# Attention with landmarks and a gated MLP: the first two loads on the hardware queues in the other order

## The chip, the cores and the metric

The kernel runs on one core of one Trainium2 chip. The metric is the device time of one execution in microseconds (us); lower is better. Of the core, the text speaks of TensorE (PE, matrix products and transposes; PEld is its weight load), VectorE (DVE), ScalarE (ACT), GpSimd (POOL) and SyncE (SP). SP and ACT each issue transfers on a hardware queue of their own, POOL on a software queue; all three queues are served by the same 16 DMA engines.

## The reference

For each of 8 batches and 8 heads, 32 landmark rows `p` attend to 576 keys and values, and the 576 queries attend to the 32 rows that come out. The result is the input of two matrix products with a gate between them.

```python
def sm_attn(qq, kk, vv):
    s = scale * np.matmul(qq, kk.transpose(0, 1, 3, 2))
    s = s - np.max(s, axis=-1, keepdims=True)
    a = np.exp(s)
    a = a / (np.sum(a, axis=-1, keepdims=True) + 1e-09)
    return np.matmul(a, vv)
p_packed = sm_attn(p, k, v)
out = sm_attn(q, p_packed, p_packed)
...
h = x @ w_in                      # 4608 x 512 by 512 x 2048
g = np.where(pos, h, np.where(neg, 0.0, (h + beta) ** 2 / (4.0 * beta)))
return (g @ w_out).astype(np.float32)
```

## The kernel before

The work goes batch by batch. For a batch: keys and queries are turned so that the head's 64 channels lie on the partitions; the landmarks' scores against the keys (`sp`), their exponentials (`ex`), the packed values and their sums (`pk`, `ppT`, `rs`); the queries' scores against the packed rows (`s`), exponentials (`eT`), sums (`sm`), logarithm and reciprocal (`ln`, `rc`) and the scaled probabilities (`A`). The packed rows are multiplied with `w_in` directly (`mp`, copied to `M`), so that the hidden layer (`h`, line 939) is a product of `M` and `A`; the gate is three steps on ACT and DVE (`x`, `t`, `hT`), and `w_out` gives the output (`o`, line 1030), which is copied to `ob` and stored. All output tiles and all hidden layers are spread over the time of the batches around them.

The order of the instructions on each engine is written out by a planner in the program (`Plan`): each step has a rank, the engines that can do it with an estimated occupancy and duration, steps that it depends on, and buffers that it takes. `plan.run` walks through time with these estimates and gives one list, in which each engine's instructions are then emitted in that order. Most ranks stand in a table (`RANKS`), by the step's name. Where the planned PE has nothing to do before the first output product, matmuls on a tile of zeros (`zeros`, line 1108) are put in; their number is fixed when the program is built. They are called fillers below. An engine works through its own list in order and waits at each instruction for what it needs.

The change touches the start of batch 0. Three kinds of loads begin there:

- On SP's and ACT's hardware queue, one half each: `p_raw`, the float32 landmarks of batches 0 and 1 (line 485, 64 KB on each queue, in runs of 256 bytes), and `k_raw`, the float32 keys of batch 0, heads 0 to 3 (line 491, 288 KB on each queue, in runs of 1536 bytes). SP brings heads 0 and 1, ACT heads 2 and 3.
- On POOL's queue, with a cast to bf16 on the way: the keys of heads 4 to 7 (line 444), then the values, queries and weights.

`p_raw` is cast by DVE to `p_nat` (line 537), turned on PE into `tpp` (line 515, eight small transposes) and copied to `pT` by ACT and DVE, two copies each. `k_raw` is cast by DVE (heads 0 and 1) and ACT (heads 2 and 3), both at line 333, into the bf16 keys. The keys of batch 0 lie in a buffer that is later used for `M`, so **the rows call the keys of batch 0 `M` too**. PE turns them in two steps of twelve transposes (line 564, `tp`): heads 0 to 3, then heads 4 to 7. Each step is copied to `kT` by ACT (one copy of 384 columns) and DVE (one of 768). The scores `sp` are two steps of twelve matmuls (line 667) of `kT` with `pT`, one after each half of `kT`; ACT makes `ex` of each (line 676). After the scores come seven fillers and then `pk` (line 735).

Of the kernel before, what the change touches and what calls it, by code (L numbers as in the profile page):

```python
# [130 lines left out]
def kernel(  # L131
# [193 lines left out]
    plan = Plan(dict(BUFS, dma=8), RANKS)  # L325
# [15 lines left out]
    def either(dve, act, *pairs, parted=None):  # L341

        def emit(e):
            for to, of in pairs:
                copy(e, to(), of(), parted)
        return {"DVE": (dve[0], dve[1], emit), "ACT": (act[0], act[1], emit)}
# [137 lines left out]
        for i, queue in enumerate((nc.sync, nc.scalar)):  # L484
            queue.dma_start(p_raw[:, i], p[i].rearrange("h n d -> n h d"))

    p_first = plan.add(-1000, {"SP": (1.0, 3.5, load_p_raw)})

    def load_k_raw(e):
        for i, queue in enumerate((nc.sync, nc.scalar)):  # L490
            queue.dma_start(k_raw[:, 2 * i:2 * i + 2], rows_of("k", 0, range(2 * i, 2 * i + 2)))

    k_first = plan.add(-999, {"SP": (1.0, 4.75, load_k_raw)}, behind=[p_first])
    casts = [plan.add(-30.2 + 0.1 * i, either(
        (0.5, 0.55), (0.8, 0.85), (lambda i=i: tokens("k", 0)[:, 2 * i:2 * i + 2], lambda i=i: k_raw[:, 2 * i:2 * i + 2])),
        [k_first], behind=landed["k", 0, 4]) for i in range(2)]
# [647 lines left out]
```

## Time and profile before

| | |
|---|---|
| time, median of 3 runs | 241.79 us (241.51 to 241.95) |
| profiled execution: its time, its span | 242.18 us, 240.4 us |
| PE busy | 233.2 us, 97% of the span |
| ACT busy | 190.0 us, 79% |
| DVE busy | 179.4 us, 75% |
| POOL busy | 37.7 us, 16% |

The span runs from the first to the last instruction of the profiled execution; its time is 1.78 us longer, for what lies around it. Busy PE counts pipelined matmuls with ends that are modelled. All times in the rows are from the start of the span.

### The profile page before, as it was taken

The numbers are of one execution on the slowest core, as the hardware profiler recorded it, in microseconds if no ns is written. First come the engines' busy times: TensorE is split into PE (matmuls) and PEld (weight loads), VectorE is DVE, ScalarE is ACT, GpSimd is POOL, SyncE is SP. The second block draws the span as 40 slices with busy tenths as digits, with TensorE's granted clock in tenths as the row PEclk, the third lists the DMA queues.
The fourth block names the chain that finished last, engine by engine and source line by source line (L and its number), as shares of the span: only waits on it lengthen the run. The fifth ranks groups of instructions, "written<-read, shape, count | busy, mean of one in ns | idle before, by whom it ended". The sixth has DMA issues, their size and how long they took to land.

```text
span 240.4 us, 5315 instructions
## 1 busy us (share of the span) xinstructions
PE 233.2 (97%) x2096; PEld 133.9 (56%) x2096; DVE 179.4 (75%) x320; ACT 190.0 (79%) x324; POOL 37.7 (16%) x57
## 2 busy tenths in 40 slices
PE   7799999999999999999999999999999999999993
PEld 3555565565555655466546655656456554654452
DVE  4549997499977996699868989999469967995000
ACT  3578898799989986899889898998789886984211
POOL 8552306000510040070005000300000000000000
PEclk9999999999999999999999999999999999999999
DMA  7999999999999999999999997989301210111315
GB/s 155 201 206 207 203 202 206 199 257 171 148 188 248 186 171 204 187 174 213 204 183 197 218 213 117 138 189 203 97 2 48 74 33 27 44 40 52 98 45 119
DMA packets 65353, 36.42 MB, mean 152 GB/s; under 512 B 34480, under 2 KB 60848, under 8 KB 65328
## 3 DMA queue, kind: packets, MB, share of 16 engines
q0 software_dynamic: 28080, 18.26, 53.5%
q1 hardware_dynamic: 36544, 17.28, 33.4%
q10 hardware_dynamic: 704, 0.56, 0.8%
q8 instruction: 16, 0.26, 0.4%
q14 instruction: 9, 0.07, 0.1%
HBM read 37.22 MB, written 9.44 MB: 194 GB/s over the span
## 4 chain that ended last, share of the span: by engine, by line
PE 92%; ACT 3%; DMA 2%; DVE 1%; issue 0%
PE o L1030 51%; PE h L939 26%; PE mp L792 3%; DMA k_raw<-in_k_dram 2%; PE o L1108 2%; PE pk L730 2%; PE sm L835 2%; PE sp L652 2%; PE s L770 1%; PE tp L564 1%; ACT M L333 1%; PE pk L740 1%; DVE M L333 0%; ACT rc L846 0%; PE tp L601 0%; PE sp L667 0%
## 5 line engine op out<-in xcount | busy, mean ns | idle before, releaser
L1030 PE MATMUL o<-w_out_sb,hT 128*128 128x512 bf16 (+1 forms) x592 | 146.3, 374 | 0.0
L960 DVE SCALAR_TENSOR_TENSOR hT<-t 128x576 bf16<-128x576 f32 (+1 forms) x130 | 91.9, 742 | 3.7 <-ACT t L955 2.1
L945 ACT ACTIVATE x<-h 128x576 f32<-128x576 f32 (+1 forms) x130 | 79.2, 646 | 11.6 <-PE h L939 10.7
L1030 PEld LDWEIGHTS <-hT 128*128 128x128 bf16 x592 | 55.3, 98 | 49.3 <-issue 5.6
L939 PE MATMUL h<-A,M 128*128 128x288 bf16 x512 | 78.1, 286 | 0.6 <-ACT M L333 0.4
L939 PEld LDWEIGHTS <-M 128*128 128x128 bf16 x512 | 49.6, 98 | 27.7 <-issue 1.5
L953 DVE TENSOR_SCALAR t<-x 128x576 f32<-128x576 f32 (+1 forms) x75 | 33.6, 463 | 10.6 <-ACT x L945 10.2
L955 ACT ACTIVATE t<-x 128x576 f32<-128x576 f32 (+1 forms) x55 | 37.0, 684 | 0.9
L333 ACT COPY ob<-o 128x512 f32<-128x512 f32 (+1 forms) x21 | 11.9, 567 | 16.5 <-PE o L1030 16.3
L851 DVE SCALAR_TENSOR_TENSOR A<-eT,rs,rc 128x576 bf16<-128x576 bf16 (+1 forms) x18 | 12.9, 747 | 10.7 <-ACT rc L846 10.7
L333 ACT CAST M<-mp 128x1024 bf16<-128x1024 f32 (+1 forms) x19 | 17.7, 969 | 2.5 <-PE mp L792 2.4
L430 POOL DMA_DIRECT2D v<-in_v_dram x14 | 10.2, 731 | 52.2 <-DVE vz L708 48.9
L430 POOL DMA_DIRECT2D kz<-in_k_dram x14 | 9.7, 701 | 50.9 <-DMA kT<-kz 50.2
L333 DVE CAST M<-mp 128x1024 bf16<-128x1024 f32 (+1 forms) x15 | 17.2, 1147 | 0.4 <-PE mp L792 0.4
L333 DVE COPY ob<-o 128x512 f32<-128x512 f32 x16 | 10.9, 685 | 2.7 <-PE o L1030 2.6
L1108 PE MATMUL o<-zeros 128*128 128x512 bf16 (+1 forms) x42 | 11.4, 405 | 1.2 <-DVE zeros L367 1.2
L828 ACT ACTIVATE eT<-s,rs 128x576 bf16<-128x576 f32 x16 | 11.1, 736 | 1.8 <-PE s L770 1.2
L841 ACT ACTIVATE ln<-sm 128x576 f32<-128x576 f32 x16 | 10.1, 651 | 1.9 <-PE sm L835 1.7
L846 ACT ACTIVATE rc<-ln 128x576 f32<-128x576 f32 (+1 forms) x18 | 10.6, 634 | 0.0
L792 PE MATMUL mp<-w_in_sb,ppT 64*32 64x512 bf16 x256 | 10.3, 380 | 0.0
L674 ACT ACTIVATE ex<-sp 128x640 bf16<-128x640 f32 x14 | 9.5, 702 | 0.3 <-PE sp L652 0.2
L444 POOL DMA_DIRECT2D q<-in_q_dram x11 | 8.4, 762 | 5.1 <-ACT x L945 2.1
(62 smaller groups left out, 110.7 us busy)
## 6 DMA issues: line engine op xcount, KB each, us to landing
out_dram<-ob SPq DMA_DIRECT2D x23, 192.0 KB, 2.7
q<-in_q_dram POOLq DMA_DIRECT2D x7, 576.0 KB, 16.1
out_dram<-ob SPq DMA_DIRECT2D x24, 128.0 KB, 3.9
kz<-in_k_dram POOLq DMA_DIRECT2D x7, 320.0 KB, 6.4
v<-in_v_dram POOLq DMA_DIRECT2D x7, 320.0 KB, 8.6
w_out_sb<-in_moe_w_out_dram POOLq DMA_DIRECT2D x4, 512.0 KB, 15.3
kz<-in_k_dram POOLq DMA_DIRECT2D x7, 256.0 KB, 7.3
v<-in_v_dram POOLq DMA_DIRECT2D x7, 256.0 KB, 9.6
```

What stands on the lines that cost most here:

```text
L333: i = (nc.vector.tensor_copy if e == "DVE" else nc.scalar.copy)(to, of)
L430: return G_.dma_start(tokens(nm, b)[p0:p0 + R5, :, :c * D], of)
L792: i = nc.tensor.matmul(have["mp", b, f][a * NP:(a + 1) * NP, g], have["ppT", b][r, g, a], w_in_sb[r, a, f * FW:(f + 1) * FW], start=True, ...
L828: nc.scalar.activation(have["eT", b, g][:, part], have["s2", b, g][:, part, :HALF], AF.Exp, scale=rs_of[b][:, g, 1:])
L851: V.scalar_tensor_tensor(have["A", b][:, g, part], have["eT", b, g][:, part], rs_of[b][:, g, :1], have["rc", b, g][:, part], ALU.mult, ALU ...
L939: nc.tensor.matmul(have["h", b, fi][:, hf, :HALF], have["M", b][:, g, fi * P:(fi + 1) * P], have["A", b][:, g, hf], start=(g == 0), stop=( ...
L945: nc.scalar.activation(have["x", b, fi][:, hs[0]:hs[-1] + 1], have["h", b, fi][:, hs[0]:hs[-1] + 1, :HALF], AF.Prelu, bias=-1.0, alpha=0.5)
L953: V.tensor_scalar(t, x, 1.0, 0.0, ALU.add, ALU.max)
L955: nc.scalar.activation(t, x, AF.Relu, bias=1.0)
L960: V.scalar_tensor_tensor(dst, t, 1.0, t, ALU.min, ALU.mult)
L1030: m = nc.tensor.matmul(have["o", key][:, :w], hT[:, fi, i * P:(i + 1) * P], w_out_sb[:, fi, cols], start=(fi == 0), stop=(fi == KF - 1))
L1108: nc.tensor.matmul(o[:, :w], zeros[:, :P], zeros[:, :w], start=True, stop=True)
```

## The change

The two loads on the hardware queues change places: the keys are planned and issued first, and the landmarks behind them. The estimated durations of the two loads, which the planner uses, change with it. No transfer, no arithmetic step and no buffer is added or removed; one line less stands in the file, so that line numbers from 489 on are one lower after the change.

```diff
-    p_first = plan.add(-1000, {"SP": (1.0, 3.5, load_p_raw)})
-
     def load_k_raw(e):
         for i, queue in enumerate((nc.sync, nc.scalar)):
             queue.dma_start(k_raw[:, 2 * i:2 * i + 2], rows_of("k", 0, range(2 * i, 2 * i + 2)))
 
-    k_first = plan.add(-999, {"SP": (1.0, 4.75, load_k_raw)}, behind=[p_first])
+    k_first = plan.add(-1000, {"SP": (1.0, 5.0, load_k_raw)})
+    p_first = plan.add(-999, {"SP": (1.0, 4.3, load_p_raw)}, behind=[k_first])
```

The planner then puts some instructions of the first ten microseconds in another order. On ACT, the start of the program read before:

```order
L310 ACT_TABLE_LOAD
L485 DMA p_raw<-in_p_dram 32x8x64
L491 DMA k_raw<-in_k_dram 96x2x384
L333 COPY pT<-tpp 64x8x32 x2
L333 CAST M<-k_raw 96x768
L333 COPY kT<-tp 128x4x96 x2
L676 ACTIVATE ex<-sp 96x12x64 x2
```

After the change ACT reads:

```order
L310 ACT_TABLE_LOAD
L489 DMA k_raw<-in_k_dram 96x2x384
L485 DMA p_raw<-in_p_dram 32x8x64
L333 CAST M<-k_raw 96x768
L333 COPY kT<-tp 128x4x96
L333 COPY pT<-tpp 64x8x32 x2
L333 COPY kT<-tp 128x4x96
L675 ACTIVATE ex<-sp 96x12x64 x2
```

The two copies of `pT` moved from ahead of the cast to between the two copies of `kT`. SP issues the same two loads in the new order too. On DVE, behind the first constants, the rows before were:

```order
L374 MEMSET ones_77 64x1
L537 CAST p_nat<-p_raw 32x1024
L333 COPY pT<-tpp 64x8x32 x2
L333 CAST M<-k_raw 96x768
L333 COPY kT<-tp 128x4x192 x2
```

and are after the change:

```order
L374 MEMSET ones_77 64x1
L333 CAST M<-k_raw 96x768
L536 CAST p_nat<-p_raw 32x1024
L333 COPY kT<-tp 128x4x192
L333 COPY pT<-tpp 64x8x32 x2
L333 COPY kT<-tp 128x4x192
```

The cast of the landmarks now stands behind that of the keys, and the copies of `pT` between those of `kT`. On PE the eight transposes of the landmarks stood ahead of all transposes of keys, behind eight fillers (seven of 512 columns and one of 256) and ahead of six more (five and one). After the change twelve fillers stand at the start, then the twelve transposes of heads 0 to 3, and then the eight of the landmarks with two fillers behind them; this is where these end and heads 4 to 7 begin:

```order
L514 LDWEIGHTS p_nat
L514 MATMUL tpp<-ident,p_nat 128x32
L1107 LDWEIGHTS zeros
L1107 MATMUL o<-zeros 128x512
L1107 LDWEIGHTS zeros
L1107 MATMUL o<-zeros 128x256
L563 LDWEIGHTS M
L563 MATMUL tp<-ident,M 128x96
```

So eight transposes of landmarks and two fillers moved between the two halves of the keys. A single filler of 256 columns, which stood between the last transpose of keys and the first score, stands between the two steps of scores instead. From there on the list of PE is the same, the seven fillers ahead of `pk` included, and so are all of POOL's list and the rest of the others.

## Rows read from the trace of the kernel before

**Rows 1.** Busy time of each engine in one long stretch (us, then instructions).

```profile
19.40:236.00 216.60, 216.03 (x1886) 124.79 (x1885) 169.29 (x290) 178.41 (x301) 25.75 (x35) 1.00 0.87 149
```

**Rows 2.** The chain that ended last: its longest piece before 20 us.

```profile
1.23 5.52 DMA k_raw<-in_k_dram
```

**Rows 3.** Timeline, the first issues of transfers: start, us, engine, line.

```profile
0.74 0.38 SPq L485 DMA_DIRECT2D p_raw<-in_p_dram  x1
0.77 0.42 ACTq L485 DMA_DIRECT2D p_raw<-in_p_dram  x1
1.19 0.43 SPq L491 DMA_DIRECT2D k_raw<-in_k_dram  x1
1.23 0.47 ACTq L491 DMA_DIRECT2D k_raw<-in_k_dram  x1
...
1.30 0.81 POOL L444 DMA_DIRECT2D M<-in_k_dram  x1 [0.85 <-POOLq L1128]
```

**Rows 4.** Transfers: size, and us from issue to landing (last number).

```profile
k_raw<-in_k_dram SPq DMA_DIRECT2D x1, 288.0 KB, 5.3
k_raw<-in_k_dram ACTq DMA_DIRECT2D x1, 288.0 KB, 5.5
M<-in_k_dram POOLq DMA_DIRECT2D x1, 288.0 KB, 6.5
```

**Rows 5.** DMA packets by queue, 2.4 to 2.6 us (q1 SP, q10 ACT).

```profile
q1 hardware_dynamic: 14, 0.02, 88.0%
q10 hardware_dynamic: 46, 0.01, 25.9%
```

**Rows 6.** The same, 5.4 to 7 us (q0 POOL's queue).

```profile
q0 software_dynamic: 424, 0.31, 128.7%
q10 hardware_dynamic: 2, 0.00, 0.4%
```

**Rows 7.** Timeline, 0 to 8 us: fillers, landmarks and the two casts of keys.

```profile
1.19 3.22 PE L1108 MATMUL o<-zeros 128*128 128x512 bf16 x8 [1.19 <-DVE zeros L367]
...
3.38 0.68 DVE L537 CAST p_nat<-p_raw 32x1024 bf16<-32x1024 f32 x1 [0.87 <-DMA p_raw<-in_p_dram]
...
4.34 0.36 PE L515 MATMUL tpp<-ident,p_nat 32*128 32x32 bf16 x8
...
4.63 1.36 PE L1108 MATMUL o<-zeros 128*128 128x512 bf16 x6
4.74 0.75 ACT L333 COPY pT<-tpp 64x256 bf16<-64x256 bf16 x2 [2.72 <-PE tpp L515]
4.74 0.58 DVE L333 COPY pT<-tpp 64x256 bf16<-64x256 bf16 x2 [0.68 <-PE tpp L515]
...
6.49 0.60 DVE L333 CAST M<-k_raw 96x768 bf16<-96x768 f32 x1 [1.17 <-DMA k_raw<-in_k_dram]
6.77 0.83 ACT L333 CAST M<-k_raw 96x768 bf16<-96x768 f32 x1 [1.28 <-DMA k_raw<-in_k_dram]
```

**Rows 8.** Timeline, 6 to 24 us: from the keys to the packed values.

```profile
7.66 1.11 PE L564 MATMUL tp<-ident,M 96*128 96x96 bf16 x22 [0.24 <-ACT M L333]
...
8.29 0.99 ACT L333 COPY kT<-tp 128x384 bf16<-128x384 bf16 x2 [0.69 <-PE tp L564]
8.29 1.07 DVE L333 COPY kT<-tp 128x768 bf16<-128x768 bf16 x2 [1.19 <-PE tp L564]
...
8.90 1.05 PE L667 MATMUL sp<-pT,kT 128*128 128x64 bf16 x24
9.48 1.50 ACT L676 ACTIVATE ex<-sp 96x768 bf16<-96x768 f32 x2 [0.20 <-PE sp L667]
...
9.79 1.68 PE L1108 MATMUL o<-zeros 128*128 128x512 bf16 x7
10.53 0.74 POOL L464 DMA_DIRECT2D w_out_sb<-in_moe_w_out_dram  x1 [1.73 <-DMA v<-in_v_dram]
...
11.40 0.94 PE L735 MATMUL pk<-ex,v 96*64 96x32 bf16 x48
```

## The prediction

> **What bounds the kernel now.** I read the stretches first, then the chain that ended last, then the timeline of the first 12 us, and last the queues. From 19.4 to 236 us PE is busy for 216.03 of 216.60 us [rows 1]: it waits for 0.6 us in nine tenths of the span, so that nothing the change leaves alone can give time back there, and what the first 19 us gain or lose arrives at the end almost one to one. In those first microseconds the chain has one long piece that is no engine's work: 5.52 us for `k_raw` [rows 2]. So the question is when the scores of batch 0 are done, and what stands between them and the load.
>
> Issued at 1.23 us, ACT's half lands 5.5 us later, at 6.73, and SP's half at 1.19 + 5.3 = 6.49 [rows 3, 4]; both casts start within 0.04 us of that [rows 7]. ACT's is the later one. I call its landing a, and count from it: the cast from a + 0.04 takes 0.83 us [rows 7]; ten transposes of heads 0 to 3 that were left follow at 7.66 = a + 0.93, and heads 4 to 7 directly behind, 22 in 1.11 us, so 0.05 us each [rows 8]. The copies of the first half start at 8.29 = a + 1.56, that is 0.13 us after the tenth, and DVE's two end at 8.29 + 1.07 = 9.36 = a + 2.63 [rows 8]. That end holds the second step of scores: 0.43 us later, at 9.79, the seven fillers begin, and `pk` follows them at 11.40 [rows 8]. The exponentials, from 9.48 for 1.50 us, are done at 10.98 and the values were there by 10.53 [rows 8]; so `pk` stands behind scores and fillers, and comes earlier or later with the end of DVE's second copy.
>
> The landmarks are far off this path: cast at 3.38, copied by 5.5 us [rows 7], while the keys come a microsecond later. That slack is what the change spends.
>
> **What the change does to the keys' landing (a).** Each half is issued where the landmarks' half was: 1.19 − 0.74 = 0.45 us earlier on SP and 1.23 − 0.77 = 0.46 on ACT [rows 3]. The keys also waited behind the landmarks' packets: between 2.4 and 2.6 us SP's queue moves packets of keys already (14 packets, 0.02 MB), ACT's still the short ones of the landmarks (46, 0.01 MB) [rows 5], 0.7 us after the keys' issue ended at 1.70. I take 0.55 us for the shift. Of the old queue almost nothing is left after 5.4 us: 2 packets on ACT's [rows 6], yet the landing comes at 6.73, so it trails the last packets by about 1.25 us. The landmarks' last packets went at about 2.6 [rows 5], and their cast began at 3.38 [rows 7]: a trail of under 0.8 us. Between the two, POOL's queue came to full flow (424 packets in 1.6 us [rows 6]). With packets that end near 4.9, a is 4.9 + 0.75 = 5.65 if the trail is the short one and 4.9 + 1.25 = 6.15 if it is the long one; I take the middle, 5.9. Outer bound on the late side: no gain, 6.73.
>
> The Trainium skill, page "DMA: Bandwidth & Descriptors", section "Queues, rings and completion order", says that a completion count is written only after all earlier writes of that DMA engine, across its queues. The two trails fit it: short when the hardware queues are alone, long beside POOL's. By it alone, with POOL's queue hardly begun at 4.9, a would be 5.65 and the keys' term below 0.25 us better; the rows don't separate the engines, and the sum keeps 5.9.
>
> **What it does to the landmarks' landing (b).** They are now last on both queues. The bytes of the two queues are the same, so their last packets go near 5.45 as before, but beside POOL's traffic. With the two trails b is 6.2 to 6.7; POOL's queue is in full flow then, so I go by the longer one and take 6.55. The late bound: 64 KB in runs of 256 bytes are 256 on each queue, 16 for each engine; POOL's 424 packets in 1.6 us [rows 6] are one for an engine every 0.06 us, and if each run lets one of them pass, 16 runs from 4.9 on last until 5.9, and b is up to 7.15.
>
> **What the new order costs.** On PE the landmarks' transposes follow heads 0 to 3, at a + 0.93 + 10 × 0.05 = a + 1.43. Until the next filler they take 4.63 − 4.34 = 0.29 us [rows 7]. The two fillers behind them are 768 columns; six fillers that were 5.5 × 512 columns took 1.36 us with their drain [rows 7], and seven full ones some 1.6 [rows 8], so 0.22 for 512 columns and 0.33 for both. Heads 4 to 7 then start at a + 2.05 instead of a + 1.43, end 12 × 0.05 later at a + 2.65, and can be copied at a + 2.78. DVE has its first copy until a + 1.56 + 0.53 = a + 2.09, the landmarks' copies for 0.58 [rows 7] until a + 2.67, and so is free: its second copy runs to a + 2.78 + 0.53 = a + 3.31, where it was a + 2.63. **The new order costs 0.68 us behind the keys' landing.** ACT: copy, 0.75 us for `pT` [rows 7], copy, so a + 1.56 + 0.5 + 0.75 + 0.5 = a + 3.31; the first scores need `pT` (a + 2.81) and take 9.48 − 8.90 = 0.58, so `ex` starts near a + 3.43 instead of a + 2.75 and ends at a + 4.93 = 10.83, still ahead of `pk`. That one filler moves between the steps of scores costs nothing: DVE's second copy ends later.
>
> If b is late, the landmarks' transposes wait: cast from b + 0.1 for 0.68, 0.06 until PE begins (as 6.49 + 0.60 to 7.15 for the keys), so b + 0.84, and DVE's second copy ends 3.31 − 1.43 = 1.88 later, at b + 2.72. A third wait is that for heads 4 to 7, which POOL brings: issued 1.30, landed 6.5 later at 7.8 [rows 3, 4]. Transposes from 7.85 give an end of 7.85 + 0.6 + 0.13 + 0.53 = 9.11. That load isn't moved by the change.
>
> **The sum.** DVE's second copy ends at the latest of a + 3.31, b + 2.72 and 9.11, against 9.36 now. With a = 5.9 and b = 6.55: 9.21, 9.27 and 9.11, so 9.27, that is 0.09 us earlier. The keys' gain of 0.83 is nearly all paid back by the 0.68 and by the landmarks, which become the last wait. On the profiled execution this makes a span of 240.3 us and a time of 242.1; that execution lies 0.39 above the median, which I take off again: **241.7 us**. Break-even is a = 6.05, b = 6.64.
>
> **The rivals.** 0.2% (0.48 us) is about what a measurement of this kernel can tell from no change.
> - *The landmarks become the long wait.* Decides from b = 6.64 on; b = 7.15 gives 9.87, 0.51 us later, 242.3. For it: short runs at the tail, beside POOL's 0.31 MB. Against it: their trail alone was under 0.8.
> - *The keys don't land earlier*, since POOL's traffic and not their place sets the trail: a between 6.5 and 6.73 gives 0.45 to 0.68 later, 242.4. Against it: nearly all their packets were through before POOL's flow.
> - *All three loads land earlier*, heads 4 to 7 too, because the hardware queues' long packets are out of POOL's way sooner: a = 5.6, b = 6.1, POOL's 0.3 us earlier, an end of 8.91, 241.3. Against it: the old 7.8 us for heads 4 to 7 stands in the way of more than 0.25.
> - *TensorE's clock falls back.* Fillers ran at 3.22/8 = 0.40 us first and at 0.22 from 4.63 on [rows 7], 512 columns at about the 1.2 and the 2.4 GHz level. Twelve fillers in one block end near 5.3, PE then idles until SP's half is cast (near 6.3), and has less to do in the next microsecond than before; before it idled for 1.16 us in the same place and kept its pace. At the lower level the nine fillers behind it (8.5 × 512 columns) cost 8.5 × 0.2 = 1.7 us, with transposes and scores 2.3 and more: 244. The page "TensorE: Matmul & The Clock Gate" of the Trainium skill, Part 1, lets the clock drop after idleness; no stretch of this trace past 4.6 us shows it.
>
> **How the numbers follow.** Forecast (an end within 0.48 us of 9.36 with a and b near the values taken): 0.63, itself 241.4 to 242.0. Landmarks late: 0.13, of which half over 0.48. Keys not earlier: 0.09. All earlier: 0.11. Clock: 0.04. Slower by over 0.2%: 0.06 + 0.09 + 0.04 = 0.19; faster: 0.11 and a little of the forecast's edge, 0.13; within: 0.68. The range, 241.2 to 242.4, holds the forecast and most of the first three rivals.
>
> **What would show it.** Right: `k_raw` landing near 5.7 and 5.9, `p_raw` after it near 6.5, the landmarks' transposes directly behind heads 0 to 3, DVE's second copy ending near 9.3, `pk` near 11.3. Wrong: a landing of `p_raw` past 6.9 or of `k_raw` past 6.3, a landing of heads 4 to 7 far from 7.8, fillers of 0.4 us after 5 us, or a change of the end that the start of `pk` doesn't show.

## The result and the profile after

The changed kernel takes 242.23 us (median of 22 executions, 241.61 to 244.32), the kernel before 241.66 beside it (22, 241.26 to 242.28). The ratio is 1.0031, with an interval of 1.0019 to 1.0043: slower by 0.3%, where 241.7 and no change were forecast (a loss of over 0.2% had a chance of 0.19). The median is 0.57 us higher; the means lie 0.77 apart, because two executions of 22 took over 244 us.

The profiled execution of the changed kernel is the shortest of its 22 (241.61 us, span 239.8), and that of before lies near the top of its range (242.18). Set side by side, these two profiles show a gain that the times don't have. First the issues in the profile after (size, us from issue to landing):

```profile
k_raw<-in_k_dram SPq DMA_DIRECT2D x1, 288.0 KB, 3.5
k_raw<-in_k_dram ACTq DMA_DIRECT2D x1, 288.0 KB, 4.3
M<-in_k_dram POOLq DMA_DIRECT2D x1, 288.0 KB, 6.0
p_raw<-in_p_dram SPq DMA_DIRECT2D x1, 64.0 KB, 4.3
p_raw<-in_p_dram ACTq DMA_DIRECT2D x1, 64.0 KB, 4.7
```

The keys are issued at 0.74 and 0.77 us now, so ACT's half lands at 5.1 (6.7 in [rows 4]); the landmarks, issued at 1.23, at 5.9; heads 4 to 7, issued at 1.30 as before, at 7.3 (7.8). The timeline of the same execution, which answers to [rows 7, 8]:

```profile
1.19 4.72 PE L1107 MATMUL o<-zeros 128*128 128x512 bf16 x12 [1.19 <-DVE zeros L367]
...
5.13 0.83 ACT L333 CAST M<-k_raw 96x768 bf16<-96x768 f32 x1 [3.11 <-DMA k_raw<-in_k_dram]
...
5.75 0.86 PE L563 MATMUL tp<-ident,M 96*128 96x96 bf16 x12
5.98 0.76 DVE L536 CAST p_nat<-p_raw 32x1024 bf16<-32x1024 f32 x1 [1.14 <-DMA p_raw<-in_p_dram]
...
6.80 0.36 PE L514 MATMUL tpp<-ident,p_nat 32*128 32x32 bf16 x8 [0.19 <-DVE p_nat L536]
...
7.43 0.68 PE L563 MATMUL tp<-ident,M 96*128 96x96 bf16 x12
...
8.14 0.56 DVE L333 COPY kT<-tp 128x768 bf16<-128x768 bf16 x1 [0.31 <-PE tp L563]
...
8.76 0.54 PE L666 MATMUL sp<-pT,kT 128*128 128x64 bf16 x12
...
10.74 0.94 PE L734 MATMUL pk<-ex,v 96*64 96x32 bf16 x48
```

The engines do what was foretold, in the foretold order: heads 0 to 3, the landmarks' transposes behind them, heads 4 to 7. DVE's second copy of `kT` ends at 8.14 + 0.56 = 8.70, `pk` starts 2.04 us later, as in [rows 8] (9.36 and 11.40). The chain now begins with the landmarks:

```profile
1.23 4.66 DMA p_raw<-in_p_dram
```

I call the end of DVE's second copy the **second copy's end**. In the eight profiles of these two kernels (table below) `pk` starts 2.04 us behind it. In six of them the time is the second copy's end + 232.8 to 233.0, in two of the changed kernel (again 1 and again 2) + 233.35. There PE waited 0.2 us more for weights from POOL's queue, at 45 or 30 us; where the other 0.3 went is not traced. So the question is where the second copy's end lies in a typical execution of each kernel.

### The profile page after: what moved, and what is told of

It is laid out like the page before. It is cut to its first block, busy times and chain, and to the rows that moved or that the text cites. A ratio compares the mean times of both kernels' runs of the same rounds, so it can differ in the third digit from the quotient of the medians.

```text
span 239.8 us, 5280 instructions
## 1 busy us (share of the span) xinstructions
PE 231.1 (96%) x2060; PEld 134.3 (56%) x2096; DVE 179.7 (75%) x320; ACT 190.1 (79%) x324; POOL 37.6 (16%) x57
## 4 chain that ended last, share of the span: by engine, by line
PE 91%; ACT 2%; DVE 2%; DMA 2%; issue 1%; DVEq 0%
PE o L1029 50%; PE h L938 27%; PE mp L791 3%; PE o L1107 2%; DMA p_raw<-in_p_dram 2%; PE sm L834 2%; PE pk L729 2%; PE sp L651 2%; PE s L769 1%; PE tp L563 1%; PE pk L739 1%; ACT M L333 1%; ACT rc L845 0%; DVE M L333 0%; PE tp L600 0%
## 5 line engine op out<-in xcount | busy, mean ns | idle before, releaser
L1029 PE MATMUL o<-w_out_sb,hT 128*128 128x512 bf16 (+1 forms) x559 | 140.1, 373 | 2.0 <-issue 0.8
```

Of the source, the lines that this page charges most:

```text
L1029: m = nc.tensor.matmul(have["o", key][:, :w], hT[:, fi, i * P:(i + 1) * P], w_out_sb[:, fi, cols], start=(fi == 0), stop=(fi == KF - 1))
```

## The experiments

The theories have letters in the expectations. A: TensorE's clock falls back. B: landings vary from one execution to the next. C: the wait that became last is the one for heads 4 to 7 on POOL's queue. D: the new order costs its 0.68 us behind the keys. E: the landmarks' short packets slow POOL's queue. F: something else slows it. G: POOL's queue is slow when it begins with no long packets of the hardware queues beside it. I: it is slow because of what the hardware queues moved just before.

**Both kernels once more, with five rounds and further profiles.** Nothing is edited.

> The changed kernel once more, for another execution in the profile. In the first profile of it the packed values (pk) start at 10.74 us, 0.66 earlier than before, and that execution took 241.61, yet the median is 242.23. Theory A (TensorE's clock): the longer executions have the same landings (k_raw by 4.3 and 5.1, p_raw near 5.9) but TensorE stays at the lower of its levels past 5.5 us or falls back to it, seen as fillers of 0.40 us for 512 columns; pk then starts at 11.4 or later at a time of 242.2 and above. Theory B (landings vary): the longer executions have p_raw or k_raw landing 0.6 us and more later, with fillers at 0.22.

> The kernel before once more; 241.3 to 242.3. Its first profile was of an execution of 242.18, 0.5 above the median, with ACT's half of k_raw landing at 6.73. Theory A: k_raw lands near 6.7 again and the median is reached with a TensorE that runs at the upper level earlier. Theory B: k_raw lands 0.5 us earlier in an execution near 241.6, with pk starting near 10.9.

> The changed kernel for one more execution in the profile. Theory C: its time goes with the landing of heads 4 to 7: near 7.3 about 241.6, near 7.9 about 242.2, near 8.4 about 242.7, with k_raw near 4.3 and 5.1 and p_raw near 5.9 in all. Theory A: the landing is near 7.3 at a time above 242, and fillers past 5.5 us take 0.40.

> As the run before it: one more execution of the changed kernel. Theory C: time = 241.6 + (landing of heads 4 to 7 minus 7.3), within 0.2 us. Theory A: no such relation.

> One more execution of the changed kernel. Theory C: its second copy of keys on DVE ends 1.33 us after heads 4 to 7 land, where that is past 7.3, and its time is that end + 232.9 within 0.3 us.

> One more execution of the kernel before. ACT's half of the keys lands near 6.0, the second copy of keys on DVE ends 2.63 us later, near 8.6, and heads 4 to 7 land between 7.0 and 7.7, too early to matter; some 1310 packets on POOL's queue from 5 to 10 us.

The repeats with rounds gave 242.29 us for the changed kernel (241.69 to 243.92, 12 executions, ratio 1.0028, interval 1.0013 to 1.0043) and 241.89 for the kernel before (11, 1.0005, 0.9996 to 1.0014). The profiles (us; a is the start of ACT's cast of keys less 0.04, the landing of heads 4 to 7 is 1.30 plus the us in its row):

| profile | a | heads 4 to 7 | second copy's end | time |
|---|---|---|---|---|
| before | 6.73 | 7.8 | 9.36 | 242.18 |
| before, again 1 | 5.97 | 7.1 | 8.60 | 241.62 |
| before, again 2 | 5.95 | 7.3 | 8.83 | 241.66 |
| after | 5.09 | 7.3 | 8.70 | 241.61 |
| after, again 1 | 5.06 | 8.3 | 9.68 | 243.02 |
| after, again 2 | 4.94 | 7.9 | 9.21 | 242.56 |
| after, again 3 | 5.19 | 7.8 | 9.16 | 241.99 |
| after, again 4 | 5.28 | 7.4 | 8.75 | 241.59 |

The first profile of before is the odd one: its keys landed 0.76 us later than in the two others. The repeats ran on three chips of the same kind (the record names none for the two first profiles), so what of a landing belongs to the chip and what to the execution is not separated here. The kernel before again, first repeat:

```profile
6.01 0.83 ACT L333 CAST M<-k_raw 96x768 bf16<-96x768 f32 x1 [0.39 <-DMA k_raw<-in_k_dram]
...
6.89 1.11 PE L564 MATMUL tp<-ident,M 96*128 96x96 bf16 x22 [0.28 <-ACT M L333]
...
7.53 1.07 DVE L333 COPY kT<-tp 128x768 bf16<-128x768 bf16 x2 [1.23 <-PE tp L564]
```

Its second copy ends at 8.60 = a + 2.63, exactly as in [rows 8] but from an earlier a. The second repeat missed the 8.6 that was expected:

```profile
4.83 2.39 PE L1108 MATMUL o<-zeros 128*128 128x512 bf16 x6
...
7.05 1.19 PE L564 MATMUL tp<-ident,M 96*128 96x96 bf16 x24
```

The same six fillers took 2.39 us instead of 1.36 and held the transposes until 7.05, though the keys were cast by 6.82; so the end is 8.83 = a + 2.88. In the changed kernel the keys don't decide. Its first repeat:

```profile
7.06 0.50 PE L1107 MATMUL o<-zeros 128*128 128x512 bf16 x2
...
8.39 0.68 PE L563 MATMUL tp<-ident,M 96*128 96x96 bf16 x12 [0.83 <-DMA M<-in_k_dram]
...
9.12 0.56 DVE L333 COPY kT<-tp 128x768 bf16<-128x768 bf16 x1 [1.31 <-PE tp L563]
```

PE stands 0.83 us at heads 4 to 7 (0.41 and 0.28 in the next two), and the second copy ends at 9.68, which is the landing (8.35) + 1.33. Its fillers end early and run at 0.22 us from 4.5 us on, so this execution is not theory A's. Landings vary (theory B), but in the longer executions of the changed kernel it is that of heads 4 to 7 that decides (theory C), not those of the keys or the landmarks. The median of the five is 9.16; the median time of before, 241.66, belongs to about 8.8.

**One half of the change at a time.** Each planner call keeps its place, but the two loads are exchanged: `order_only` has the new order of the engines with the landmarks first on the queues, `queue_only` the old order of the engines with the keys first.

```diff
# order_only, in the changed kernel
-    k_first = plan.add(-1000, {"SP": (1.0, 5.0, load_k_raw)})
-    p_first = plan.add(-999, {"SP": (1.0, 4.3, load_p_raw)}, behind=[k_first])
+    k_first = plan.add(-1000, {"SP": (1.0, 5.0, load_p_raw)})
+    p_first = plan.add(-999, {"SP": (1.0, 4.3, load_k_raw)}, behind=[k_first])
# queue_only, in the kernel before
-    p_first = plan.add(-1000, {"SP": (1.0, 3.5, load_p_raw)})
+    p_first = plan.add(-1000, {"SP": (1.0, 3.5, lambda e: load_k_raw(e))})
-    k_first = plan.add(-999, {"SP": (1.0, 4.75, load_k_raw)}, behind=[p_first])
+    k_first = plan.add(-999, {"SP": (1.0, 4.75, load_p_raw)}, behind=[p_first])
```

> The engines' order of the changed kernel, but the landmarks issued first on both hardware queues, as before. The prediction's term for the new order alone is 0.68 us behind the landing of the keys: 242.3 with landings as before (pk near 12.0 in the profile when k_raw lands at 6.7). Theory A: the spread of the changed kernel (up to 244) is seen here too, since it has the same PE list and the keys come later still. Theory B: the spread of the kernel before.

> The queues' order of the changed kernel, but the engines' order of the kernel before. DVE and ACT then wait for the landmarks (landing near 5.9) and their copies before they cast the keys: casts done near 8.7 instead of 7.6, so 1.1 us slower, 242.8. Theory A: PE idles for some 2.5 us ahead of the transposes of keys, so that executions with the lower clock are more frequent, 244 and more. Theory B: 242.8 with a spread of half a microsecond.

`order_only` took 242.25 us (242.1 to 244.12, 11; ratio 1.0027, 1.0012 to 1.0042):

```profile
5.99 0.83 ACT L333 CAST M<-k_raw 96x768 bf16<-96x768 f32 x1 [3.97 <-DMA k_raw<-in_k_dram]
...
8.04 0.68 PE L563 MATMUL tp<-ident,M 96*128 96x96 bf16 x12
...
8.75 0.56 DVE L333 COPY kT<-tp 128x768 bf16<-128x768 bf16 x1
```

With a = 5.95 and no wait for heads 4 to 7 (landed at 7.6) the second copy ends at 9.31 = a + 3.36, against a + 2.63 in the repeat of before with the same a. The order's price was 0.73 where 0.68 was worked out: theory D holds.

`queue_only` took 244.54 us (244.4 to 245.08, 4; 1.012, 1.0105 to 1.0134):

```profile
1.19 3.38 PE L1108 MATMUL o<-zeros 128*128 128x512 bf16 x8 [1.19 <-DVE zeros L367]
...
6.71 0.39 PE L515 MATMUL tpp<-ident,p_nat 32*128 32x32 bf16 x8 [2.14 <-DVE p_nat L537]
7.04 2.53 PE L1108 MATMUL o<-zeros 128*128 128x512 bf16 x6
...
7.91 0.83 ACT L333 CAST M<-k_raw 96x768 bf16<-96x768 f32 x1
...
9.35 2.13 PE L564 MATMUL tp<-ident,M 96*128 96x96 bf16 x24
```

Every engine stands at its landmarks' instruction while the keys lie ready. After PE's wait of 2.14 us the six fillers take 2.53 us and the 24 transposes 2.13, against 1.36 in [rows 7] and 1.11 for 22 in [rows 8]: half pace. `pk` starts at 14.29. The time is theory A's (244 and more), not the 242.8 of the waits alone. So the new order of the engines is needed for the new order on the queues, and it alone costs as much as the whole change.

**Without the wait for heads 4 to 7.** The second twelve transposes read heads 0 to 3 again, in the changed kernel and in the one before; batch 0's scores of heads 4 to 7 are then those of heads 0 to 3, and the load still runs.

```diff
-    have[nm, b][:, hs[j], X * c:X * (c + 1)].rearrange("p c d -> p (c d)"),
+    have[nm, b][:, hs[j] % 4 if (nm, b) == ("k", 0) else hs[j], X * c:X * (c + 1)].rearrange("p c d -> p (c d)"),
```

> The changed kernel, in which the second twelve transposes of keys read heads 0 to 3 again, so that the keys of heads 4 to 7, still loaded by POOL, are left out of the result and nothing waits for them. Theory C (the wait that became the last one is that for heads 4 to 7, whose landing varies from 7.3 to 8.4 us between executions): the loss goes, since DVE's second copy of keys then ends by the landmarks' landing (5.9 + 2.72 = 8.6): 241.6, and the spread up to 244 shrinks. Theory A (TensorE's clock): 242.2 and the spread stay. Theory D (the new order's 0.68 us): 242.2 stays.

> The same edit in the kernel before (heads 4 to 7 left out, heads 0 to 3 turned twice). Theory C: there the keys' half on ACT is last (landing near 6.0), heads 4 to 7 mostly in time, so at most 0.2 us faster: 241.5. Theory A and D: 241.65, no change.

The changed kernel came to 241.94 us (241.57 to 243.57, 11; 1.0015, 1.0001 to 1.003) where 241.6 was expected: by the ratio about half of the loss is gone, though the intervals overlap; the kernel before to 241.65 (12; 0.9998, 0.9988 to 1.0008), no difference. That the changed kernel waits for heads 4 to 7 is shown by its profiles (0.83, 0.41 and 0.28 us in three of five), so theory C holds for such executions. By the medians the wait costs it some 0.3 us, which these times alone don't prove, and it isn't the whole; the kernel before loses nothing by it.

**The landmarks' packets.** In `after_long_p` and `before_long_p` the landmarks come in 32 runs of 2048 bytes per queue instead of 256 of 256, and lie in another arrangement; in `after_no_p` DVE writes a constant in their place.

```diff
-            queue.dma_start(p_raw[:, i], p[i].rearrange("h n d -> n h d"))
+            queue.dma_start(p_raw[:, i].rearrange("n h d -> n (h d)"), p[i].rearrange("h (n c) d -> (h n) (c d)", c=8))
# after_no_p: the load itself is replaced
+        V.memset(p_raw.rearrange("n i h d -> n (i h d)"), 0.1)
```

> The changed kernel with the landmarks loaded in 32 runs of 2048 bytes on each queue instead of 256 runs of 256 bytes: the same bytes, but the rows of a head lie otherwise in the tile, so that the landmarks are mixed up in the result. Theory E (the short packets of the landmarks, which now fall on the first packets of POOL's queue, slow that queue, and heads 4 to 7 and the weights behind them land later): POOL's queue moves some 1320 packets from 5 to 10 us as in the kernel before instead of 1120 to 1275, heads 4 to 7 land by 7.5, 241.7. Theory F (POOL's queue is slowed by something else in the new order): 1120 to 1275 packets, 242.2.

> The changed kernel without the load of the landmarks of batches 0 and 1: DVE fills their tile with a constant instead, so these landmarks are left out of the result. Nothing waits for their landing, and their packets are gone. Theory E: POOL's queue as in the kernel before (some 1320 packets from 5 to 10 us), heads 4 to 7 by 7.4, 241.5. Theory F: heads 4 to 7 near 7.9 still, 242.1. If the landing of the landmarks at 5.9 were what matters: 241.3, with pk near 10.5.

> The kernel before with the same long runs for the landmarks (mixed up in the result likewise). There the landmarks' packets go before POOL's first ones, so theory E expects no change of POOL's queue; the keys behind them start some 0.2 us earlier at most: 241.4 to 241.7. Theory F: the same.

`after_long_p` took 242.13 us (241.85 to 245.44, 11; 1.0029, 1.0005 to 1.0052), with heads 4 to 7 at 7.8 and PE waiting 0.48 for them; `after_no_p` 241.95 (12; 1.0006, 0.9995 to 1.0017), so that most of the loss is gone, with heads 4 to 7 at 7.2; `before_long_p` 241.56 (11; 0.999, 0.9982 to 0.9999).

Packets of POOL's queue between 5 and 10 us, from each profile: the kernel before 1317, 1349 and 1307, `order_only` 1306, `before_long_p` 1262; the changed kernel 1275, 1118, 1210, 1226 and 1281, `after_long_p` 1140, `after_no_p` 1168. On each of the four chips that the record names, every profile with the keys first on the queues lies below every one with the landmarks first. But the stretch matters: from 0 to 10 us the kernel before has 1356, 1408 and 1384, the changed kernel 1369, 1221, 1332, 1282 and 1349, `after_long_p` 1236, and `after_no_p` 1385, because 217 of its packets go ahead of 5 us. So in most executions POOL's queue has moved less by 10 us with the keys first. It does so with long runs too (`after_long_p`), so that the packets are short is not needed for it. Without the landmarks' load the queue is where it is in the kernel before, in packets by 10 us, in the landing of heads 4 to 7 and nearly in time, as theory E would have it; only the packets from 5 to 10 us are as theory F would have them. So theory E doesn't hold as far as it names short packets; whether the landmarks' load as such slows POOL's queue, one profile of each kernel doesn't settle.

**Neither landmarks nor heads 4 to 7; and no keys on the hardware queues.** `after_no_m_no_p` joins the two edits above; `before_no_k` replaces the load of `k_raw` by a constant written by DVE.

```diff
# before_no_k
-            queue.dma_start(k_raw[:, 2 * i:2 * i + 2], rows_of("k", 0, range(2 * i, 2 * i + 2)))
+        V.memset(k_raw.rearrange("p h d -> p (h d)"), 0.1)
```

> The changed kernel with both waits taken away: heads 4 to 7 left out (heads 0 to 3 turned twice) and the landmarks left out (their tile filled with a constant by DVE). Theory C with the landmarks beside it (the end of DVE's second copy is the latest of the keys' landing + 3.31, the landmarks' + 2.72 and that of heads 4 to 7 + 1.33): only the keys are left, 5.1 + 3.31 = 8.4 against 8.6 in a typical execution of the kernel before, so 241.5, 0.1% faster, where each alone left 0.06 and 0.15% slower. Theory A or D: at or above 242.

> The kernel before without the load of the float32 keys (filled with a constant by DVE, so heads 0 to 3 of the keys of batch 0 are left out). The hardware queues are then done at 2.6 us, long before POOL's first packets. Theory G (POOL's queue flows slower when it begins beside no long packets of the hardware queues): 1120 to 1275 packets on it from 5 to 10 us. Theory I (it flows slower because of traffic of the hardware queues just before it): 1310 and more.

`after_no_m_no_p` took 241.93 us (241.35 to 243.75, 12; 1.0024, 1.0004 to 1.0044), a miss. Its timeline shows the next thing in the way:

```profile
1.19 5.09 PE L1107 MATMUL o<-zeros 128*128 128x512 bf16 x12 [1.19 <-DVE zeros L367]
6.07 0.95 PE L563 MATMUL tp<-ident,M 96*128 96x96 bf16 x12
```

The twelve fillers ran at 0.42 us each on average until 6.28, though ACT's half had landed at 4.7, so the second copy ended only at 8.85, where 8.4 was expected. Heads 4 to 7 landed at 7.2 here, and POOL's queue had moved 1388 packets by 10 us: again without the landmarks' load, and again as in the kernel before. Three of its twelve executions took 243.2 to 243.8 us at a mean granted clock of 0.993. `before_no_k` (241.79, one profile) brought heads 4 to 7 at 5.6 and 1355 packets of POOL's queue between 5 and 10 us: a queue that begins alone isn't slow in this execution, which speaks against theory G.

**The clock.** Of 91 executions of the kernels with the new order of the engines so far, eight show a mean granted clock of 0.989 to 0.993, and they took 243.2 to 244.3 us, the two over 244 of the changed kernel among them; of 132 with the old order none lies below 0.996. Executions of kernels that ran once are left out of these counts, and so is `queue_only` (old order, keys first), of whose four executions two show 0.993, at 244.46 and 244.62.

This mean counts less than it seems to. In every one of the twenty traces the records of the clock begin only where PE's pace doubles, from 0.43 to 0.22 us for 512 columns: at 4.1, 4.4 and 6.9 us in the three profiles of before, between 4.1 and 6.2 in the five of the changed kernel, at 12.5 in `queue_only`. A stretch ahead of the first record reads 1.00. So a late rise of the clock leaves the mean at 1.00, and only a fall lowers it; means of 0.997 to 0.999 come, in the profiles, from the end of the span alone, where PE has nothing left to do. The eight are therefore the least number of executions that the clock held up. Others are as long at a high mean (242.99 and 243.14 us of the changed kernel at 1.000, 245.44 of `after_long_p` at 0.998); none of these was profiled. Three kernels with other fillers in the changed kernel: the first block is 8 or 16 of 512 columns instead of 11 and a half, or the two behind the landmarks are left out.

```diff
         at = t.start + t.ways["PE"][0]
+    fill[0] = (fill[0][0], 16)     # after_first8;  32 in after_first16
+    fill[1] = (fill[1][0], 0)      # after_second0, this line alone
```

> In this kernel the first block of fillers is 8 of 512 columns instead of 11 and one of 256, all else as after the change; with about 0.40 us each they end near 4.5 us, so that PE waits longer for the keys. Theory A (what the longest runs lost is TensorE's clock, which falls back when PE waits in these first microseconds): more than half of the runs above 243 with a mean granted clock of 0.994 or less, a median of 243.3 or more, and in the profile transposes or fillers at half pace behind 5 us. Theory C (the waits for loads alone): the fillers were done before the keys in most executions anyway, so the median stays at 242.0 to 242.4, the mean clock at 0.996 or more in nine of ten runs as in the changed kernel.

> The first block of fillers is 16 of 512 columns, all else as after the change; at 0.40 us and then 0.21 us each they end between 6.0 and 7.3 us, so PE hardly waits before the transposes of heads 0 to 3. Theory A: no run with a mean clock of 0.994 or less; but the transposes start with the fillers' end, so DVE's second copy ends at about that end + 2.5, 8.7 to 9.8, and the median is 242.0 to 242.9. Theory C: the same median, and about one run in ten at a clock of 0.994 or less, as in the changed kernel; so the median tells only the price of the fillers, and the clocks of the runs tell the theories apart as far as 11 runs can.

> The two fillers behind the landmarks' transposes (768 columns, 0.33 us) are left out, all else as after the change. Theory A with the wait ahead of heads 4 to 7 as the place where the clock falls back: more runs than one in ten above 243 with a mean clock of 0.994 or less. Theory C: nothing, since the wait for heads 4 to 7 stands there; median 242.0 to 242.3, and where that load is early at most 0.3 us less.

| kernel | median (range, executions) | ratio | at a clock of 0.991 or less |
|---|---|---|---|
| `after_first8` | 243.29 (242.82 to 244.94, 6) | 1.0083 (1.0056 to 1.0111) | 3 of 6, 243.1 to 243.4 |
| `after_first16` | 242.63 (242.17 to 243.12, 6) | 1.0036 (1.0022 to 1.005) | 0 of 6, all at 1.000 |
| `after_second0` | 242.36 (241.79 to 243.79, 12) | 1.0034 (1.0017 to 1.0052) | 2 of 12, 243.77 and 243.79 |

The profile of `after_first8` fell on one of the three. Its busy time by stretch (PE, PEld, DVE, ACT, POOL, then the granted clock):

```profile
5.00:7.00 2.00, 1.24 (x21) 0.94 (x22) 1.10 (x3) 1.18 (x2) 2.00 (x4) 1.00 1.25 174
7.00:8.40 1.40, 1.11 (x22) 0.75 (x21) 0.83 (x4) 0.79 (x4) 0.78 (x2) 1.00 1.22 173
8.40:8.80 0.40, 0.40 (x11) 0.35 (x7) 0.40 (x1) 0.40 (x1) 0.25 (x1) 0.50 1.30 202
...
10.80:11.20 0.40, 0.40 (x2) 0.15 (x1) 0.38 (x2) 0.00 (x0) 0.00 (x0) 0.50 1.33 202
11.20:12.00 0.80, 0.80 (x3) 0.28 (x2) 0.00 (x0) 0.00 (x0) 0.74 (x2) 0.62 1.31 199
```

and its timeline:

```profile
1.19 3.60 PE L1108 MATMUL o<-zeros 128*128 128x512 bf16 x8 [1.19 <-DVE zeros L367]
...
5.13 0.26 PE L563 MATMUL tp<-ident,M 96*128 96x96 bf16 x2 [0.34 <-DVE M L333]
...
6.02 0.60 PE L563 MATMUL tp<-ident,M 96*128 96x96 bf16 x10 [0.63 <-ACT M L333]
...
7.65 0.69 PE L563 MATMUL tp<-ident,M 96*128 96x96 bf16 x12 [0.29 <-DMA M<-in_k_dram]
...
8.37 0.56 DVE L333 COPY kT<-tp 128x768 bf16<-128x768 bf16 x1 [0.53 <-PE tp L563]
...
8.99 0.85 PE L666 MATMUL sp<-pT,kT 128*128 128x64 bf16 x12
...
12.31 0.87 PE L734 MATMUL pk<-ex,v 96*64 96x32 bf16 x43
```

The granted clock is 0.50, the lower level of 1.2 GHz, from 8.4 to 11.8 us by the trace's record, after PE had stood three times (0.34, 0.63 and 0.29 us). The second copy ends at 8.93, but `pk` starts 3.38 us behind it instead of 2.04: 1.34 us to the clock. That shows theory A for this execution; of the six, three show the low mean, where more than half were expected, and the median is 243.29, where 243.3 or more was. In the changed kernel it is inferred: the same low mean clock and the same excess, in two of 22 executions, none of them profiled. The place isn't settled: in the profile of `after_second0` PE stood 1.89 us ahead of heads 4 to 7, and the next twelve scores took 0.53 us, full pace:

```profile
8.85 0.68 PE L563 MATMUL tp<-ident,M 96*128 96x96 bf16 x12 [1.89 <-DMA M<-in_k_dram]
9.37 0.53 PE L666 MATMUL sp<-pT,kT 128*128 128x64 bf16 x12
```

`after_first16` has no wait there, all its executions at full clock, and pays with fillers that end at 7.47 us, later than the keys. Three of the six executions of `after_first8` took 242.8 to 244.9 at a mean clock of 0.998 or more; what held those up was not profiled. A rise as late as that of `queue_only`, whose mean clock is 1.000, would look like this; it is not shown.

## Why the prediction was wrong

**The formula was right, its deciding term was not.** The prediction said that the second copy's end is the latest of a + 3.31, b + 2.72 and the landing of heads 4 to 7 + 1.3, and that it reaches the end one to one. In the profile after that is 8.40, 5.88 + 2.72 = 8.60 and 8.6; measured 8.70. In its first repeat the third decides, 8.35 + 1.31 = 9.66; measured 9.68. The prediction expected the landmarks to be the last wait; in three of the five profiles it is heads 4 to 7.

**The forecast of that end came close by luck.** It was 9.27; the median of five profiles is 9.16. But the terms behind it, 9.21 for the keys and 9.27 for the landmarks, came to about 8.4 and 8.6. Both landings were earlier than their bounds: a is 4.9 to 5.3 (forecast 5.9, bounds 5.65 to 6.15) and b about 5.9 (forecast 6.55). With the long packets first the two hardware queues move 0.57 MB between 2 and 4 us (0.41 to 0.50 in three profiles of before), and ACT's queue has no packet of landmarks after 4.75, where 5.45 was assumed. The place in the queue is not what brought ACT's keys forward: their first packet goes at 2.6 us in the first profiles of both kernels, their last at 5.4 before and 4.1 after. The gain was lost at the floor, 9.11 in the prediction, that heads 4 to 7 set. The 7.8 us that it took for their landing is the median of the five, by luck too: it came from the first profile of before, and the two repeats of before have 7.1 and 7.3.

```profile
q10 hardware_dynamic: 198, 0.29, 48.6%
q1 hardware_dynamic: 228, 0.28, 43.4%
```

These are the packets of the profile after between 2 and 4 us. The landmarks' landing at 5.9 trails their last packets (ACT's, at 4.75) by some 1.1 us, with POOL's queue in flow. That looks like the prediction's long trail, but in the two repeats of before the keys' landing trails their last packets (at 5.3) by 0.7 us, with POOL's queue in flow as well. So a short trail without POOL's queue and a long one beside it, as the prediction read it, is not what more profiles show. By the Trainium skill, page "DMA: Bandwidth & Descriptors", section "Queues, rings and completion order", a completion waits for earlier writes of its engine. No run here separates the engines, so none shows it or speaks against it.

**The step that failed is the base of the sum: "against 9.36 now", and then "that execution lies 0.39 above the median, which I take off again".** The excess of that execution over the median was no constant beside the change: it lay in the very wait that the change replaces. Its keys landed at 6.73, in the two repeats of before at 5.97 and 5.95. The median of before belongs to an end of about 8.8 (8.60 and 8.83 in the two repeats), so 9.27 is 0.4 to 0.5 later and not 0.09 earlier. To take 0.39 off the result as well was to count a late landing as a gain of the change. Without that, the prediction's own 9.27 gives 9.27 + 232.85 = 242.1, and 242.23 was measured.

**Where the keys' gain went.** The keys come 0.9 us earlier than in a typical execution of before. 0.7 goes to the new order of the engines (`order_only`). The remaining 0.2 goes to the landmarks and heads 4 to 7 where these are early (ends of 8.70 and 8.75), and where heads 4 to 7 are late, in three of five profiles, they add 0.4 to 1.0 (9.16 to 9.68). That "that load isn't moved by the change" was doubtful: it landed at 7.3 to 8.3 in the five profiles after and 7.1 to 7.8 in three of before, and POOL's queue moved fewer packets between 5 and 10 us in each of the five than in any of the three (by 10 us in four of the five). The short packets don't account for that and theory G hardly does; the landmarks' load itself, theories F and I stay open.

**The rivals.** "TensorE's clock falls back" had a chance of 0.04 for the whole kernel, at 244; by the mean clock it happens in two of 22 executions at least, at 244.16 and 244.32, and these carry 242.43 − 242.25 = 0.18 of the 0.77 us between the means. The prediction found no fall in the trace of before past 4.6 us; there is one, from 239.6 us on, behind PE's last work, where it costs nothing. The Trainium skill, page "TensorE: Matmul & The Clock Gate", Part 1, lets the clock drop after idleness; the end of that trace agrees (0.50 granted), and `after_first8` has a drop behind short waits, while the wait of 1.89 us in `after_second0` went by without one. "The landmarks become the long wait" is true of the profile after, whose chain starts with them, at no price. "All three loads land earlier" is what that profile and the fourth repeat show against the first profile of before (against its repeats heads 4 to 7 are no earlier), and they only reach the time of before (241.61 and 241.59).

## What to carry to other kernels

When the profiled execution lies above the median, find which wait was long in it before it becomes the base of a sum; further profiles of the unchanged kernel tell it (here two were enough). If the change removes that very wait, the excess belongs to the base. A load that is brought forward gains only until the next one on another queue; put the floor of every load beside the gain, with the spread of its landing over several executions. A block of fillers of fixed number is part of such a change: too short and PE's clock can fall, too long and the fillers hold up what has landed.

## What the runs showed of the hardware

The landing of one and the same load varies by more than this change is worth: heads 4 to 7, issued at 1.30 us in every profile, landed between 7.2 and 8.8 with the keys first on the other queues (7.2 in `after_no_p`, 8.8 in `after_second0`), and between 7.0 and 7.8 with the landmarks first (5.6 without the float32 keys). These profiles lie on several chips; two executions of the changed kernel on one chip had 7.8 and 7.9.

Half pace of PE in the first microseconds is the lower level of its clock, though the views read 1.00 there. The first fillers of each kernel take 0.43 us for 512 columns, and so do those of `after_first8` where the record shows 0.50; later ones take 0.22. In `queue_only` the six fillers behind the wait of 2.14 us (2.53 us) and the transposes behind them still go at half pace, and the view reads:

```profile
8.00:10.00 2.00, 2.00 (x13) 1.11 (x12) 0.31 (x1) 0.74 (x1) 0.64 (x1) 1.00 1.30 197
```

That is the busy time from 8 to 10 us; the first record of the clock in this trace begins at 12.5 us, and 1.00 ahead of it stands for no record. When the pace doubles varies between executions of one kernel: at 4.1, 4.4 and 6.9 us in the three profiles of before. The twelve first fillers of the changed kernel took 4.72 us in its profile and, with nothing else altered ahead of them, 4.16 in that of `after_second0`. So pace is read from the duration of equal matmuls, not from the granted clock alone.
